# Two heads side by side on half-arrays, and another order of the late value products, in a windowed attention with a gated MLP on one core

## The chip, the cores and the metric

One core of a Trainium2 chip. The metric is the device time of one execution in microseconds; the median of three runs stands for a kernel. TensorE (PE) multiplies, PEld is its weight load, VectorE is DVE, ScalarE is ACT, GpSimd is POOL, and SyncE is SP, which issues the DMAs. A profiled execution has a span, a little shorter than its device time.

## The reference

```python
batch, n_heads, seq, head_dim = (4, 8, 768, 64); n_sink, window = (4, 128)     # q, k, v: float32
scores = (1 / sqrt(D)) * q @ k.T
keep = (pos_k < n_sink) | ((pos_q - pos_k >= 0) & (pos_q - pos_k < window))
scores = where(keep, scores, -1e9); scores -= max(scores)
a = exp(scores); a = a / (sum(a) + 1e-9)
x = (a @ v).transpose(0, 2, 1, 3).reshape(3072, 512)
h = x @ w_in            # w_in  [512, 2048]
g = h * cos(h)
out = g @ w_out         # w_out [2048, 512], float64 like w_in (it arrives as pairs of int32)
```

A query attends to the 128 keys up to its own and to the first four. Each row of 512 outputs of eight heads goes through the gated MLP.

## The kernel before

**Tiling.** The 3072 rows are cut in 12 chunks of 256 queries: first the four chunks that start a batch (`i0 == 0`), then the other eight. A chunk has eight heads, so there are 96 heads in order; the first 32 are called early. Early heads need no sinks of their own: their keys are the 256 of their own rows. The other 64, the late heads, see three blocks of 128 keys and 8 sink columns (`SW` = 136). Two chunks, 16 heads, make one dense pair of 512 rows: x in two float32r parts (`xhi`, `xlo`), three products each with `whi_in`, `wlo_in` into `h` (L476), the gate on ScalarE and VectorE, and three products into four accumulators (L521). There are six dense pairs of 16 slots, each slot 12 products of L476 and 12 of L521 with 512 moving columns.

**What runs beside what.** Heads 0 to 15 come first, alone. The first dense pair then runs among heads 16 to 31, the next four among 16 late heads each, and the last alone. While the first heads and the first dense pair run, the weights are loaded and turned from float64 pairs to float32 and split in two (`weight_piece`: L583, L589, L595 on VectorE, L616 on ScalarE, L619), through two raw buffers.

**An early pair of heads.** Two heads' q and k come in by DMA side by side, 64 columns each, and are turned on TensorE (`pe_turn`, L931) into one PSUM bank: head one on rows 0 to 63, head two on rows 64 to 127. `q_out` copies each head's 64 rows of q to its own half of `env.tqe`, whose other halves are zero (`early_q`, a memset); `k_out` copies both heads' k. `scores_pe` (L968) multiplies, in fp32, per head and query block, q with zeros on 64 of the 128 rows against the k of both heads: 128 columns for the first query block, 256 for the second. `mask` (L1046) adds the mask and takes the least, `expo` (L1055) exponentiates with a running sum, `denom` and `norm` divide the weights. `turn_early` (L1146) turns the three weight blocks of a head on TensorE, `p_out` copies them out of PSUM, and `values_pe` (L1191) multiplies them, in fp32, by v with 64 columns of zeros (`early_v`), so that both heads of a pair add into one 128-row tile. For the first 16 heads `split_early` takes x_hi from that tile, subtracts it inside PSUM with a product by minus the identity (L354) and copies the rest as x_lo. Heads 16 to 31 turn their weights in two steps and keep each head's 64 rows (`x_keep`).

**A late head.** Weights and v are split in float32r parts; `values` (L1215) makes seven products into `o.av`: the v operand has 128 columns (both parts) for the high weights and 64 for the low ones. The sinks of four heads are gathered by VectorE in `gc` (`sink_cols`, L1105, L1107), turned (L1120), and multiplied by 128 columns of sink values from `vs_part` (L1095, L1096). Rows 64 to 127 of the result are added to rows 0 to 63 (L1222, L1234).

**What sets the order.** Nothing is left to a run-time scheduler. Each step is added to a `Plan` with its engines and costs, its dependences, its buffers (`buf(tag, n)`) and a due time made of the constants in `C`. `Plan.order` goes through a model of the five engines once and emits the steps in a fixed order for each queue. A step with several engines listed goes to one of them there. PSUM has eight banks: `b0` to `b4`, `s`, `tp`, `av`.

## Time and profile before

| | |
|---|---|
| median of 3 runs | 727.12 us (726.59 to 727.43) |
| span of the profiled execution | 725.6 us |
| TensorE busy (records, tails in them) | 708.8 us, 3674 matmuls |
| VectorE, ScalarE, GpSimd busy | 599.3, 527.7, 127.5 us |
| first dense matmul | 55.7 us |
| TensorE clock granted | 1.00 of full speed in all stretches but the last |

The profiled execution's own time is its span and about 1.5 us around it: the median of the runs is 1.55 us above the span. Matmul records overlap: each one lasts from its start to the modelled end of the pipeline, so that the time a matmul takes from the engine is read from its start to the start of the next. An fp32 matmul leaves two records, a transpose or a float32r matmul one. Line numbers are those of the kernel before.

### The profile page before, as it was taken

The page shows a single profiled execution, that of the slowest core. Times are in us where ns is not written, and L with a number is a line of the kernel's source. Part 1 is how long each engine was busy: PE and PEld are TensorE (multiplying, and loading weights), DVE is VectorE, ACT ScalarE, POOL GpSimd, SP SyncE. Part 2 cuts the span into 40 slices and gives each one's busy share as a digit, 9 for nine tenths or more (in the row PEclk, how much of TensorE's full clock was granted, in tenths as well). Part 3 has the DMA queues.
Part 4 walks back from the last instruction along what each step waited for, and adds up shares of the span by engine and source line. Part 5 has one row for each costly group of instructions (what it writes and reads, how often), then busy time and mean ns, then how long its engine had stood idle before and what let it go on. Part 6 is the DMA issues. An engine that isn't in the chain of part 4 may idle for free.

```text
span 725.6 us, 12986 instructions
## 1 busy us (share of the span) xinstructions
PE 708.8 (98%) x3674; PEld 584.1 (81%) x3674; DVE 599.3 (83%) x1849; ACT 527.7 (73%) x1344; POOL 127.5 (18%) x213
## 2 busy tenths in 40 slices
PE   7998999999999999999999999999999999999996
PEld 7766787888888888888888888888888888888884
DVE  6889998988988978988978988878989865667762
ACT  3896976788697697796686886776887766566642
POOL 1010000001223222232231222232123222100000
PEclk9999999999999999999999999999999999999999
DMA  5665555533256333355433254433254500375551
GB/s 144 182 186 153 158 162 162 141 65 68 68 118 146 73 62 57 72 119 124 93 60 59 56 131 103 118 61 64 43 139 99 119 18 12 97 210 148 164 137 64
DMA packets 236501, 77.13 MB, mean 106 GB/s; under 512 B 221060, under 2 KB 221060, under 8 KB 236420
## 3 DMA queue, kind: packets, MB, share of 16 engines
q1 hardware_dynamic: 236128, 75.15, 43.4%
q10 hardware_dynamic: 292, 1.05, 0.5%
q8 instruction: 32, 0.52, 0.3%
q14 instruction: 49, 0.40, 0.2%
HBM read 69.86 MB, written 6.29 MB: 105 GB/s over the span
## 4 chain that ended last, share of the span: by engine, by line
PE 81%; ACT 11%; DVE 4%; issue 2%; DMA 1%; SPq 0%; ACTq 0%; DVEq 0%
PE acc L521 32%; PE h L476 32%; PE av L1215 5%; PE s L1024 4%; ACT p L1055 3%; PE s L968 2%; PE av L1191 2%; PE tp L1136 2%; ACT p L1073 1%; PE tp L1146 1%; PE qk L931 1%; ACT L485 1%; PE idle L1532 1%; ACT L1055 1%; ACT early L390 1%
## 5 line engine op out<-in xcount | busy, mean ns | idle before, releaser
L521 PE MATMUL acc<-whi_out,ghi 128*128 128x512 f32 x384 | 161.8, 421 | 0.0
L476 PE MATMUL h<-xhi,whi_in 128*128 128x512 f32 x384 | 155.2, 404 | 0.0
L476 PE MATMUL h<-xlo,whi_in 128*128 128x512 f32 x384 | 150.9, 393 | 0.0
L521 PE MATMUL acc<-whi_out,glo 128*128 128x512 f32 x384 | 150.8, 393 | 0.0
L521 PE MATMUL acc<-wlo_out,ghi 128*128 128x512 f32 x384 | 150.1, 391 | 0.0
L476 PE MATMUL h<-xhi,wlo_in 128*128 128x512 f32 x384 | 150.0, 391 | 0.0
L1174 POOL TENSOR_SCALAR_AFFINE_SELECT ph<-ph 128x512 fp32r<-128x512 f32 x128 | 87.4, 683 | 230.3 <-DVE ph L1167 226.4
L485 ACT ACTIVATE r<-h 128x512 f32<-128x512 f32 x96 | 57.1, 598 | 48.6 <-PE h L476 46.0
L476 PEld LDWEIGHTS h<-xlo,whi_in 128*128 128x128 f32 x384 | 72.1, 188 | 16.3
L521 PEld LDWEIGHTS acc<-whi_out,glo 128*128 128x128 f32 x384 | 72.1, 188 | 16.2
L476 PEld LDWEIGHTS h<-xhi,whi_in 128*128 128x128 f32 x384 | 72.2, 188 | 12.0 <-DVE r L498 0.3
L476 PEld LDWEIGHTS h<-xhi,wlo_in 128*128 128x128 f32 x384 | 72.4, 189 | 11.2
L521 PEld LDWEIGHTS acc<-whi_out,ghi 128*128 128x128 f32 x384 | 72.8, 190 | 10.7
L521 PEld LDWEIGHTS acc<-wlo_out,ghi 128*128 128x128 f32 x384 | 72.7, 189 | 9.4
L1055 ACT ACTIVATE p<-p,st 128x136 f32<-128x136 f32 (+1 forms) x192 | 79.2, 416 | 0.3
L498 DVE SCALAR_TENSOR_TENSOR r<-r,h 128x512 f32<-128x512 f32 x96 | 64.6, 674 | 16.9 <-ACT r L491 16.1
L506 ACT CAST ghi<-r 128x512 fp32r<-128x512 f32 x96 | 59.5, 619 | 22.8 <-PE acc L521 15.7
L512 DVE TENSOR_TENSOR glo<-r,ghi 128x512 fp32r<-128x512 f32 x96 | 66.3, 691 | 7.1 <-ACT ghi L506 6.3
L1046 DVE CUSTOM_DVE_ANT_0 p<-s,mk 128x136 f32<-128x136 f32 (+1 forms) x192 | 59.8, 313 | 6.5 <-PE s L968 3.1
L984 ACT CAST l<-tq 64x256 fp32r<-64x256 f32 x64 | 25.8, 403 | 46.7 <-PE s L1024 46.4
L1032 DVE COPY_PREDICATED s<-mk,s 128x128 f32<-128x128 int32 x128 | 37.3, 291 | 24.6 <-PE s L1024 22.5
L1024 PEld LDWEIGHTS s<-r,l 128*128 128x128 f32 x256 | 46.5, 188 | 12.3 <-DVE ph L1167 1.5
(153 smaller groups left out, 1302.3 us busy)
## 6 DMA issues: line engine op xcount, KB each, us to landing
xk<-in_k_dram SPq DMA_DIRECT2D x256, 48.0 KB
raw<-in_moe_w_out_dram SPq DMA_DIRECT2D x16, 512.0 KB
wt<-in_moe_w_in_dram SPq DMA_DIRECT2D x32, 256.0 KB
raw<-in_moe_w_in_dram SPq DMA_DIRECT2D x14, 512.0 KB
v<-in_v_dram SPq DMA_DIRECT2D x64, 96.0 KB
raw<-in_v_dram SPq DMA_DIRECT2D x32, 192.0 KB
out_dram<-wt SPq DMA_DIRECT2D x22, 256.0 KB
wt<-in_moe_w_out_dram SPq DMA_DIRECT2D x20, 256.0 KB
```

Of the source, the lines that this page charges most:

```text
L476: nc.tensor.matmul(out=o.h, lhsT=w[:, c, fs], rhs=xx[:, c, :], start=(c == 0 and n == 0), stop=(c == NC - 1 and n == 2),)
L485: nc.scalar.activation(out=o.r, in_=o.h, func=AF.Sin, scale=0.5)
L498: nc.vector.scalar_tensor_tensor(out=o.r, in0=o.r, scalar=0.5, in1=o.h, op0=ALU.subtract, op1=ALU.mult)
L506: nc.scalar.copy(out=o.ghi, in_=o.r)
L512: e.tensor_tensor(out=o.glo, in0=o.r, in1=f32(o.ghi), op=ALU.subtract)
L521: nc.tensor.matmul(out=y.acc[j], lhsT=gg[:, j * P : (j + 1) * P], rhs=w[:, f, :], start=(f == 0 and n == 0), stop=(f == NFT - 1 and n == 2),)
L1024: nc.tensor.matmul(out=o.s_ps[j][:, :w], lhsT=o.l[:, j * P : (j + 1) * P], rhs=r.rearrange("p n s -> p (n s)")[:, c0 : c0 + w], start=(n = ...
L1032: nc.vector.copy_predicated(out=o.s_ps[j][:, :P], mask=below.bitcast(I32), data=o.s_ps[j][:, SW : SW + P])
L1046: nc.vector.tensor_tensor_reduce(out=o.pj[j][:, :w], in0=o.s_ps[j][:, :w], in1=masks[min(o.i0 + j, 2)][:, :w], op0=ALU.add, op1=ALU.min, s ...
L1055: nc.scalar.activation(out=o.pj[j][:, :w], in_=o.pj[j][:, :w], func=AF.Exp, bias=o.lead.st[:, 0, o.nth, j : j + 1], scale=-1.0, accum_out= ...
L1174: nc.gpsimd.affine_select(out=ph[:, :, b, :], in_=f32(ph)[:, :, 1, :], pattern=[[0, 2 * CB], [(-1, 1)[b], P]], compare_op=(ALU.is_gt, ALU. ...
L1215: nc.tensor.matmul(out=dst, lhsT=lhs, rhs=rhs, start=(n == 0), stop=(n == len(seq) - 1), skip_group_check=True)
```

## The change

Early heads: the scores of two heads are issued as one step, alternating between the heads. Each uses the 64 rows of q and k that are its own, and each head's scores go to a PSUM bank of its own (`s` and `b0`, or `s` and `tp`). The values of two heads are one step too: v without zeros has 64 columns, and the two heads write partitions 0 to 63 and 64 to 127 of one bank. The zeros, their memsets and the two half copies of q go; q, k and v of a pair have two buffers each. x_lo is one subtraction on VectorE, in place of the product by minus the identity and a copy. Heads 16 to 31 turn their weights in one step and keep both heads' rows in one copy. The division of the weights is as before, ahead of the turn; its place in the plan and the cost given for the exponential of early heads change.

Late heads: the seven products come in another order, the sink values have 64 columns, with high and low parts on rows of their own (`odd16` marks the rows of the low part), and the sink columns are gathered twice, 32 for a head instead of 16. The sink values of a batch are loaded with eight DMAs instead of four.

All constants of the planner but a few are new, so that the order of nearly all steps can differ.

```diff
-    "ALT": 1.986, "BLF": 0.62, "CK": 43.221, "DA": -1.397, "DH": -1.402, "DM": -1.278, "DQ": 3.964, "DS": -6.226,
+    "ALT": 3.451, "BLF": 0.803, "CK": 48.478, "DA": -6.513, "DH": -5.89, "DM": -3.062, "DQ": 6.689, "DS": -21.639,
...
-    def x_lo(y, p, cs, early):
-        def fn(e):
-            if early:
-                copy(e, xlo[:, p, cs], y.f(p, cs))
-            else:
-                e.tensor_tensor(out=xlo[:, p, cs], in0=y.f(p, cs), in1=f32(xhi)[:, p, cs], op=ALU.subtract)
+    def x_lo(y, p, cs):
+        def fn(e):
+            e.tensor_tensor(out=xlo[:, p, cs], in0=y.f(p, cs), in1=f32(xhi)[:, p, cs], op=ALU.subtract)
...
-        m = add([("PE", 0.12)], x_minus(y, p, cs), [i], t + 0.3)
-        env.minus.users.append(m)
-        j = add([("ACT", act(NT, False)), ("DVE", dve(NT))], x_lo(y, p, cs, True), [m], t + 0.6)
+        j = add([("DVE", dve(NT))], x_lo(y, p, cs), [i], t + 0.6)
...
-                    for dup in range(2):
+                    for dup in range(4):
...
+        def q_out(o):
+            def fn(e):
+                o.tq = env.tqe[o.btq.nth]
+                copy(e, o.tq, o.qk[:, 0])
+            return fn
...
+        def scores_pe(pair):
+            oe = pair[0]
+
+            def fn(e):
+                for o in pair:
+                    t = ps.tile([P, 3 * P], F32, name=f"s_{o.tag}", tag=o.s_tag)
+                    o.s_ps = [t[:, : o.ws[0]], t[:, o.ws[0] : o.ws[0] + o.ws[1]]]
+                for j in range(CB):
+                    for o in pair:
+                        r = slice(o.odd * 64, o.odd * 64 + 64)
+                        c0 = max(o.i0 + j - 1 - o.kb0, 0) * o.sw
+                        nc.tensor.matmul(
+                            out=o.s_ps[j], lhsT=oe.tq[r, j * P : (j + 1) * P],
+                            rhs=oe.tk.rearrange("p n s -> p (n s)")[r, c0 : c0 + o.ws[j]], start=True, stop=True,
+                        )
+            return fn
...
+                e.tensor_copy(out=w, in_=o.vs32[r])
+                e.tensor_scalar(out=w, in0=f32(w), scalar1=odd16[r], scalar2=1.0, op0=ALU.mult, op1=ALU.mult)
+                e.tensor_tensor(out=w, in0=f32(w), in1=o.vs32[r], op=ALU.add)
...
+        def values_pair(pair, x):
+            oe = pair[0]
+
+            def fn(e):
+                av = x.f[oe.pair] = ps.tile([P, NT], F32, name=f"av_{oe.tag}", tag=oe.av_tag)
+                for n, (kb, qs) in enumerate(oe.cols):
+                    for o in pair:
+                        nc.tensor.matmul(
+                            out=av[o.odd * 64 : o.odd * 64 + 64, (qs[0] - oe.i0) * P : (qs[-1] + 1 - oe.i0) * P],
+                            lhsT=oe.v32[:, kb - oe.kb0, o.odd], rhs=o.pt[:, oe.offs[n] * P : oe.offs[n + 1] * P],
+                            start=(n == 0), stop=(n == len(oe.cols) - 1), skip_group_check=True,
+                        )
+            return fn
...
-                seq = [wide_hi]
-                if o.sj:
-                    lhs = sink_values()[:, o.pair, o.odd].rearrange("p a d -> p (a d)")
-                    seq.append((o.av[:, o.sj[0] * P :], lhs, gt[:, : len(o.sj) * P]))
-                seq += [*narrow[:2], wide_lo, *narrow[2:]]
+                sinks = o.av[:D], sink_values()[:, o.h // 4, o.pair % 2, o.odd], gt
+                seq = [
+                    block(0, o.phi, 2 * D), block(0, o.plo, D), sinks, block(2, o.phi, 2 * D),
+                    block(2, o.plo, D), block(1, o.plo, D), block(1, o.phi, 2 * D),
+                ]
...
-                r = slice(o.odd * 64, o.odd * 64 + 64)
-                copy(e, x.y.f(o.pair, slice(x.n * NT, x.n * NT + NT))[r], x.f[o.pair][r])
+                copy(e, x.y.f(o.pair, slice(x.n * NT, x.n * NT + NT)), x.f[o.pair])
...
-            o.s_tag = ("s", "b0") if g < GA else ("s", "s")
+            o.s_tag = ("s", "b0" if g < GA else "tp")[o.odd]
...
-                o.tp_tag, o.av_tag = "s" if o.comb else "tp", "tp"
+                o.tp_tag, o.av_tag = ("s", "tp") if o.comb else (("s", "tp")[o.odd], "s")
...
-                    bx, bb, o.btq = buf("xq", 1), buf(o.qk_tag, 1), buf("tqe", 1)
+                    bx, bb, o.btq = buf("xq", 1), buf(o.qk_tag, 1), buf("tqe", 2)
```

`block(n, t, w)` is the product of key block n by the weights `t` with the first w columns of its v operand.

## Rows read from the trace of the kernel before

**Rows 1.** The page: busy us (share), count; dense matmuls: busy us, mean ns.

```profile
PE 708.8 (98%) x3674; PEld 584.1 (81%) x3674; DVE 599.3 (83%) x1849; ACT 527.7 (73%) x1344; POOL 127.5 (18%) x213
...
L521 PE MATMUL acc<-whi_out,ghi 128*128 128x512 f32 x384 | 161.8, 421 | 0.0
```

**Rows 2.** Busy time by stretch of the span, all engines; then clock, DMA share, GB/s.

```profile
16.00:63.50 47.50, 43.87 (x256) 34.77 (x255) 42.31 (x142) 38.54 (x127) 3.48 (x5) 1.00 0.67 177
63.50:180.40 116.90, 115.16 (x573) 92.48 (x573) 107.55 (x292) 90.49 (x228) 2.55 (x7) 1.00 0.50 129
180.40:622.00 441.60, 440.42 (x2361) 366.56 (x2361) 376.41 (x1228) 337.99 (x876) 119.29 (x190) 1.00 0.38 83
...
sum 30.00, PE 27.78 PEld 21.38 DVE 26.68 ACT 28.22 POOL 2.48; mean PE 9.26 PEld 7.13 DVE 8.89 ACT 9.41 POOL 0.83
```

**Rows 3.** The chain that ended last, from 16 to 63.5 us, shares by line.

```profile
by line: PE s L968 13.8%; PE av L1191 12.3%; ACT early L390 8.4%; DMA raw<-in_moe_w_out_dram 7.9%; ACT p L1055 5.8%; PE qk L931 5.6%; DVE wt L589 5.4%; PE tp L1146 4.4%; ACT p L1073 4.2%; DVE wt L595 4.2%; issue 4.0%; PE idle L1532 3.5%; DV
```

**Rows 4.** Timeline of TensorE: one late head's values (start, duration; xN merges N records).

```profile
325.63 0.28 PE L1215 MATMUL av<-ph,vr 128*128 128x256 f32 x1
325.75 0.28 PE L1215 MATMUL av<-gt,x1r 128*128 128x256 f32 x1
325.87 0.22 PE L1215 MATMUL av<-ph,vr 128*128 128x128 f32 x1
...
325.92 0.40 PE L1215 MATMUL av<-ph,vr 128*64 128x128 f32 x3
325.99 0.40 PE L1215 MATMUL av<-ph,vr 128*64 128x256 f32 x3
326.10 0.28 PE L1215 MATMUL av<-ph,vr 128*128 128x128 f32 x2
326.16 0.22 PE L1215 MATMUL av<-ph,vr 128*64 128x128 f32 x1
326.22 0.45 PE L521 MATMUL acc<-whi_out,ghi 128*128 128x512 f32 x1
326.50 0.39 PE L521 MATMUL acc<-wlo_out,ghi 128*128 128x512 f32 x1
326.73 0.40 PE L521 MATMUL acc<-whi_out,glo 128*128 128x512 f32 x1
```

**Rows 5.** Groups by line and shape: busy us, mean ns, idle before; one DMA issue.

```profile
L1105 DVE CAST gc<-p 128x16 fp32r<-128x16 f32 x64 | 7.4, 174 | 1.9 <-ACT p L1073 1.9
L390 ACT COPY early<-qk 64x256 f32<-64x256 f32 x20 | 7.3, 366 | 11.0 <-PE qk L931 10.5
L390 ACT COPY early<-tp 128x384 f32<-128x384 f32 x13 | 6.2, 476 | 3.2 <-PE tp L1146 1.9 <-PE av L1191 1.2
L392 DVE COPY early<-tp 128x256 f32<-128x256 f32 x7 | 3.0, 421 | 0.4 <-PE tp L1146 0.4
...
1.31 0.46 SPq L923
```

**Rows 6.** Timeline of TensorE: an early head's scores and values among dense matmuls.

```profile
80.87 0.38 PE L968 MATMUL s<-tk,early 128*128 128x128 f32 x2
81.09 0.38 PE L1146 MATMUL tp<-ident,p 128*128 128x128 f32 x2
...
84.24 0.59 PE L968 MATMUL s<-tk,early 128*128 128x256 f32 x2
84.67 0.81 PE L1191 MATMUL av<-early,vpe 128*128 128x256 f32 x4
85.24 0.48 PE L476 MATMUL h<-xhi,whi_in 128*128 128x512 f32 x1
85.56 0.39 PE L476 MATMUL h<-xhi,wlo_in 128*128 128x512 f32 x1
```

**Rows 7.** Timeline of VectorE from 62 us, with the weight DMA it waits for.

```profile
62.45 0.43 DVE L583 TENSOR_SCALAR wt<-raw 128x512 int32<-128x512 int32 x1 [0.28 <-DMA raw<-in_moe_w_out_dram]
...
65.29 0.42 DVE L392 COPY early<-qk 64x256 f32<-64x256 f32 x1
```

More of the change, by code (lines that the diff above doesn't have):

```diff
@@ L1117, in fn @@
             def fn(e):
-                o.gp = late_bank(o, 2)[:GR]
-                for n, j in enumerate(o.sj):
-                    nc.tensor.transpose(
-                        out=o.gp[:, n * P : (n + 1) * P], in_=gc[:, j], identity=ident,
-                    )
+                o.gp = late_bank(o, 2)
+                for j in range(CB):
+                    nc.tensor.transpose(out=o.gp[:, j * P : (j + 1) * P], in_=gc[:, j], identity=ident)
             return fn
@@ L1408, in softmax @@
             ready = [i for _, o in group for i in o.msk]
-            ex = [
-                add(
-                    [("ACT", act(o.w[j]) + 0.19)], expo(o, j), ready, t + 1.02 * n + 0.01 * j, table="exp"
-                )
-                for n, (_, o) in enumerate(group) for j in range(CB)
-            ]
+            ex = []
+            for n, (_, o) in enumerate(group):
+                o.nm = [
+                    add(
+                        [("ACT", act(o.w[j]) + (0.0 if o.early else 0.19))], expo(o, j), ready, t + 1.02 * n + 0.01 * j,
+                        table="exp",
+                    )
+                    for j in range(CB)
+                ]
+                ex += o.nm
             t += 1.02 * (len(group) - 1) + 0.5
@@ new lines, in after_softmax @@
+            if o.early:
+                if o.odd == 0:
+                    return
+                pair = oe, _ = heads[g - 1], o
+                te = head_time(g - 1)
+                oe.bxv, bpt = buf("ve", 2), buf("phi", 1)
+                hold = [early[2:], [early_end]][g // 2] if g < 4 else []
+                v0 = add(dma(2), load_v_pair(oe), [oe.bxv, *hold], te - 2 * T + C["DV"] + 3.2, lat=2.4)
+                ready = [v0]
+                for m, w in enumerate(pair):
+                    pt = buf(w.tp_tag, 1)
+                    p0 = add([("PE", 0.107 * o.n)], turn_early(w), w.nm + [pt], head_time(g - 1 + m) + C["DA"] + 1.3)
+                    w.bp.users.append(p0)
+                    both = [("ACT", act(o.n * P, False)), ("DVE", dve(o.n * P))]
+                    p1 = add(both, p_out(w), [p0, ready[1] if m else bpt], head_time(g - 1 + m) + C["DA"] + 1.8)
+                    pt.users.append(p1)
+                    ready.append(p1)
+                bav = buf(oe.av_tag, 1)
+                y0 = add([("PE", 0.84)], values_pair(pair, x), [*ready, bav], te + C["DA"] + 5.0)
+                for bb in (oe.bxv, bpt, *early[2:]):
+                    bb.users.append(y0)
@@ L1616, in banded_path @@
             waiting.append((g, o))
-            if behind:
-                after_softmax(*behind.pop(0))
+            if behind and (behind[0][1].comb or o.odd != o.comb):
+                for _ in range(1 if behind[0][1].comb else 2):
+                    after_softmax(*behind.pop(0))
             if len(waiting) == o.nq:
```

298 lines of the change are left out of this document (118 added, 180 removed), and 12 rows, old and new, of the table C.

## The prediction

> **What bounds the kernel now.** I read the shares of the engines first, and they show TensorE busy for 98% of a span of 725.6 us [rows 1]. Busy time alone is no bound, since a matmul's record holds its pipeline's tail: the 512-column records of one group last 421 ns in the mean [rows 1], yet dense matmuls start 0.23 us apart [rows 4]. So I read start against start. The table of stretches [rows 2] cuts the kernel where the work changes. From 180.4 to 622 us TensorE is busy 440.42 of 441.60 us: there the last wait is always TensorE's own queue, and what a matmul group loses or gains there moves the end by as much. From 63.5 to 180.4 us, where the first dense pair runs among heads 16 to 31, TensorE is busy 115.16 of 116.90 and VectorE 107.55. From 16 to 63.5 us, heads 0 to 15 alone, no engine is: TensorE 43.87 of 47.50 with its tails and fillers, VectorE 42.31, ScalarE 38.54, but ScalarE takes 28.22 of the 30 us from 20 to 50 [rows 2]. The chain there goes from engine to engine: scores of L968 13.8%, values of L1191 12.3%, ScalarE's copies 8.4%, a weight DMA 7.9% [rows 3]. From 622 us on nothing of the change runs.
>
> **Late values (heads 32 to 95, 64 heads).** One head starts its products at 325.63, .75, .87, .92, .99, 326.10, .16, and the next dense matmul at 326.22, whose follower comes 0.28 later instead of 0.23 [rows 4]. That is 0.59 + 0.05 = 0.64 us. The steps are 0.12 after each 256-column matmul, 0.06 after a 128-column one whose successor has 64 weight columns, and 0.11 after the last one, whose successor has 128 (0.06 of it seen as start, 0.05 as the late follower). So a short matmul hides a 64-column weight load and not a 128-column one. The old order is wide, wide sink, 128, 64, 64, 128, 64: four steps of 0.12 and three of 0.06, 0.64 with rounding. The new order is 128 columns by 128 weights, 128 by 64, 256 sink columns by 64, 128 by 128, 128 by 64, 256 by 64, 256 by 128: steps 0.06, 0.06, 0.12, 0.06, 0.06, 0.12, 0.12, together 0.59. That is 0.055 less a head, 3.5 us for 64, all on TensorE's queue: **-3.5 us**. The bounds are 0, if the steps after the sinks follow their columns in some other way, and -4.5, if only the columns counted (1280 of them at 0.23 us for 512, 0.575 a head).
>
> The sinks' widening is paid on VectorE: 128 instructions for the sink columns, the casts at 174 ns, write 32 elements instead of 16 (from 16 elements at 174 ns to 256 at 421 it is 1.03 ns an element, so +17 ns each, 2.1 us), and there are 16 more instructions on the sink values, each at most a 256-column copy's 0.42, 6.7 us [rows 5]. VectorE has 65 us idle in that stretch [rows 2], which hides these 9; without that cover they would be at most +9. The four extra sink-value DMAs a batch take 0.46 us each of SP's queue [rows 5], 7.4 us over the whole stretch; queued behind them are only the key and query loads of heads some steps off. I cost them at nothing.
>
> **Scores and values of the first 32 heads (16 pairs).** These are full fp32, two records a matmul. A 128-column pair of records takes 0.22 us (80.87 to 81.09), a 256-column pair 0.43 (84.24 to 84.67) [rows 6], so 0.66 a head and 1.32 a pair of heads. The values of a head take 0.57 + 0.09 = 0.66 in the same rows, 1.31 a pair. The old kernel pads with zeros: 128 rows or columns of which 64 work. The new one issues as many columns, on half-arrays. No trace here has two matmuls on different halves, so I bound it. If nothing overlaps, the gain is 0. If everything does, 0.66 for each group. In between, matmuls start in order: the first head's two records follow each other on one half, the second head's first record can start only when the first head's second does, and so on. By passes of 0.11 and 0.22 the four matmuls then take 0.88. If moreover each 128-column weight load takes the 0.11 that it costs where it is not hidden [rows 4], one after the other, the scores take 1.10. I take 0.99 for scores (-0.33) and 0.88 for values (-0.43; their loads have 64 columns), nearest to the rows on in-order starts.
>
> From 63.5 to 180.4 us that is 7 pairs of scores and 8 of values, 2.3 + 3.4 = 5.7 us. VectorE is at 92% there and loses only copies: query copies 128 rows high instead of two of 64 (366 ns on ScalarE; 32 become 16), the kept values likewise (16 become 8), the transposed weights in one copy of 384 columns (476) instead of two, which saves one instruction's fixed 174 - 17 = 157 ns [rows 5]. Their ScalarE and VectorE time falls by some 16 x 0.37 + 8 x 0.37 + 16 x 0.16 = 11.4 us, 3 of it VectorE's in this stretch. Weight pieces hold VectorE back too: at 62.45 and again before 65.3 it stands in line behind a raw weight DMA, and a query copy behind it [rows 7]. So I give 80%: **-4.6 us**.
>
> From 16 to 63.5 us scores are 6.6 and values 5.8 us of the chain; a quarter and a third of them is 3.5. ScalarE, the fullest engine from 20 to 50, loses half of its 64-row query copies (1.7 us) and, to VectorE, the low halves of x. The subtraction by matmul (L354) goes as well. Against it, the first mask of a pair now waits for both heads' scores and the values for both heads' weights, about 0.5 us later each; the second query and key buffer lets the next pair start ahead of that. I take **-3 us**, bounds 0 and -6. The memsets and the x_lo moved to VectorE lie in gaps there, at nothing. The new priorities reorder everything; I know no sign for that, and allow 4 us either way.
>
> Sum: 3.5 + 4.6 + 3.0 = 11.1. The profiled span of 725.6 us becomes 714.5. The median of the runs is 1.5 us above that span, so the forecast is **716.0 us**.
>
> **The rule that speaks against it.** The rows of a late head switch four times between matmuls of 128 and of 64 weight columns, and the steps of 0.06 leave no room for a stall [rows 4]. The Trainium skill, TensorEngine Tiling (Array Packing), section Key Properties, says that a change of tiling mode drains TensorE. For column widths at one position this case's trace disagrees; for row halves, and for a second column position, no run here shows it. By that rule the time would be the slower rival's, 735; by the rows on widths it would be the sum's.
>
> **Rivals.** (1) *The halves overlap fully* or the new order closes the idle time as well: 0.66 for each group, -1.3 a pair. Eight pairs among the dense work give 8 to 10, the first 16 heads 5 to 6, the late values 3.5: about 709. For it: different halves share no weights; against it: starts in order, and ScalarE at 94% in the first stretch. (2) *Halves run one after the other*: the change doesn't do what it says. Then -3.5 from the late values and 1 to 2 from the copies remain: 722. For it: fp32 takes two records each, which no row shows overlapped. (3) *VectorE becomes the bound* between 63.5 and 180.4: with 92% there, and the weight conversions in its queue ahead of the masks, the early gain is lost and the late extra 9 us on VectorE delay some scores: 724 to 727. (4) *Slower: a drain at every switch.* Two fp32 records of 128 columns, 0.11 apart, end 0.38 after the first one's start, 0.16 after the next group may start [rows 6], so a drain costs up to 0.16, and 0.12 for a load that can't be hidden [rows 4]: 0.28. Each pair switches four times (into and out of row halves, into and out of column halves), 1.1 us. With the overlap lost too, eight pairs add 9 among the dense work and up to 5 in the first stretch; less 3.5 and 1.5 of the copies, about 735. It decides from 0.19 us a switch on, where it eats the pair's 0.76, and turns the whole slower from about 0.25.
>
> **How the numbers follow.** Forecast (partial overlap, 711 to 720) 0.47; rival 1 0.17; rival 2 0.13; rival 3 0.11; rival 4 0.12. Slower by over 0.2% (728.6 on; about what a measurement can tell from no change) is rival 4 and a little of rival 3: 0.13. Within 0.2%: part of rival 3, 0.05. Faster: 0.82. Leaving out the far ends of rivals 1 and 4, the range is 706 to 727.5.
>
> **What would show it.** Late values: the sum of steps per head 0.59 instead of 0.64, the sink matmul 128*64. Early scores and values: starts of the second head's records beside the first's, and a pair's four matmuls in 0.9 to 1.1 us and 0.9; a drain would stand as a gap of 0.15 us or more ahead of the first record of a group and behind its last. Stretches: heads 0 to 15 shorter by 3, the first dense pair by 4 to 5, each later dense pair by 0.9. I am wrong if the early groups take 1.3 us a pair, or if VectorE's idle time between 63 and 180 us goes to nothing while TensorE waits.

## The result, and the profile after

The changed kernel takes 731.1 us (median of 4 runs, 729.6 to 731.9) against 726.9 for the kernel before on the same chip: ratio 1.0058, 95% interval 1.0044 to 1.0072. It is 4 us slower, where the prediction had it 11 us faster. Its profiled span is 727.9 us. The page's shares, then the table of stretches, cut at the first matmuls of the first, second and sixth dense pair (us, then busy time and count of PE, PEld, DVE, ACT, POOL, granted clock, DMA share, GB/s):

```profile
PE 699.0 (96%) x3666; PEld 555.5 (76%) x3666; DVE 600.8 (83%) x1844; ACT 523.5 (72%) x1335; POOL 129.1 (18%) x200
...
16.00:51.50 35.50, 27.83 (x199) 18.02 (x197) 27.35 (x110) 30.00 (x106) 2.34 (x5) 0.95 0.64 167
51.50:167.40 115.90, 113.19 (x588) 82.79 (x589) 104.75 (x270) 88.67 (x212) 5.77 (x8) 1.00 0.55 145
167.40:624.60 457.20, 449.34 (x2388) 365.82 (x2387) 396.84 (x1282) 344.92 (x905) 119.77 (x178) 1.00 0.39 84
```

Against [rows 1, 2]: TensorE is busy for 10 us less in a longer span. The 0.95 in the first row is a fall of the granted clock to 0.74 (part of it at 1.2 GHz) from 45 to 51.5 us, behind 5 us with TensorE busy for 3.67; before shows 1.00 there. What that costs is not shown; behind it the clock is 1.00 in both. The first dense pair starts at 51.5 us instead of 55.7, and the second at 167.4 instead of 180.4. The sixth starts at 624.6 instead of 622.3. So the change is ahead by 13.0 us at the second dense pair, and the stretch behind it, which the prediction called TensorE-bound, takes 457.2 instead of 441.9 us and gives all of it back. Of the 13.0, 4.5 are work that only moved: behind the second pair's start stand 15 more output matmuls of 0.231 us and 8 more late scores. The real lead is 8.5.

To follow the rest I use one number, **TensorE's idle between pairs**: over all matmuls from the second dense pair's first to the sixth's, the time between two starts less the step that the matmul's form shows (0.45 ns a column, from 0.23 us for 512, or 0.92 ns a column of the next weights where that is more, from 0.12 us for 128; [rows 4]). It is 2.6 us before and 16.7 after. A change in the third digit of these two rates moves all of these sums together by about 1 us; the differences between kernels stay. The account closes: +4.5 moved, -3.5 late products, +14.1 idle make +15.1, and 15.3 were measured.

What the prediction said of the late values came. One late head's values (timeline of TensorE):

```profile
330.49 0.40 PE L514 MATMUL acc<-whi_out,glo 128*128 128x512 f32 x1
330.73 0.28 PE L1192 MATMUL av<-ph,vr 128*128 128x128 f32 x2
330.85 0.28 PE L1192 MATMUL av<-gt,vs 128*64 128x256 f32 x1
330.96 0.52 PE L1192 MATMUL av<-ph,vr 128*128 128x128 f32 x4
331.32 0.39 PE L514 MATMUL acc<-whi_out,ghi 128*128 128x512 f32 x1
```

330.73 to 331.32 is 0.59 us, and the follower comes in the usual 0.23. An early pair's scores and values (the first line of each group merges all eight records of two heads; the line of x2 is a narrow window at the group's start):

```profile
81.77 0.40 PE L514 MATMUL acc<-whi_out,glo 128*128 128x512 f32 x1
82.10 0.38 PE L954 MATMUL s<-early 64*128 64x128 f32 x2
...
82.10 0.93 PE L954 MATMUL s<-early 64*128 64x128 f32 x8
82.95 0.49 PE L469 MATMUL h<-xhi,whi_in 128*128 128x512 f32 x1
83.29 0.39 PE L469 MATMUL h<-xhi,wlo_in 128*128 128x512 f32 x1
...
89.02 0.40 PE L514 MATMUL acc<-whi_out,glo 128*128 128x512 f32 x1
89.35 0.87 PE L1167 MATMUL av<-early,early 128*64 128x256 f32 x8
90.15 0.50 PE L469 MATMUL h<-xhi,whi_in 128*128 128x512 f32 x1
90.49 0.39 PE L469 MATMUL h<-xhi,wlo_in 128*128 128x512 f32 x1
```

The two heads' records start 6 to 7 ns apart (0, 6, 213, 220, 325, 331, 543, 550 ns from the group's first): the halves overlap fully. But the dense matmul ahead of the group holds the queue for 0.33 us instead of 0.23, and so does the one behind it. From dense start to dense start, less two dense steps, a pair's scores take 1.52 - 0.46 = 1.06 us and its values 1.01, where the kernel before takes 1.32 and 1.31 [rows 6].

All six score groups between dense matmuls take 1.06. Of the eight value groups there only four take 1.01. In the others the second head's first record stands 0.04 to 0.66 us behind the first head's, because its weights are still being copied out of PSUM, and they take 1.04, 1.30, 1.42 and 1.66; the mean of the eight is 1.18. The longest, with the copy it waits for:

```profile
163.54 1.52 PE L1167 MATMUL av<-early,early 128*64 128x256 f32 x8
163.60 0.54 DVE L385 COPY early<-tp 128x384 f32<-128x384 f32 x1
165.00 0.50 PE L514 MATMUL acc<-whi_out,ghi 128*128 128x512 f32 x1
```

### The profile page after: what moved, and what is told of

Its sections match the earlier page's. It is cut to its first block, busy times and chain, and to the rows that moved or that the text cites. A ratio compares the mean times of both kernels' runs of the same rounds, so it can differ in the third digit from the quotient of the medians.

```text
span 727.9 us, 12978 instructions
## 1 busy us (share of the span) xinstructions
PE 699.0 (96%) x3666; PEld 555.5 (76%) x3666; DVE 600.8 (83%) x1844; ACT 523.5 (72%) x1335; POOL 129.1 (18%) x200
## 4 chain that ended last, share of the span: by engine, by line
PE 73%; ACT 10%; DVE 9%; DMA 3%; issue 3%; SPq 1%; DVEq 0%; ACTq 0%
PE h L469 29%; PE acc L514 28%; PE s L1010 4%; PE av L1192 4%; ACT p L1041 3%; DMA xk<-in_k_dram 2%; PE tp L1120 2%; PE s L954 1%; PE idle L1506 1%; ACT p L1059 1%; DMA xq<-in_q_dram 1%; ACT early L383 1%; DVE glo L505 1%; DVE p L1032 1%; SPq L877 1%
## 5 line engine op out<-in xcount | busy, mean ns | idle before, releaser
L514 PE MATMUL acc<-whi_out,ghi 128*128 128x512 f32 x384 | 155.5, 405 | 0.0
L1154 POOL TENSOR_SCALAR_AFFINE_SELECT ph<-ph 128x512 fp32r<-128x512 f32 x128 | 90.0, 703 | 237.5 <-DVE ph L1147 213.3
L478 ACT ACTIVATE r<-h 128x512 f32<-128x512 f32 x96 | 57.1, 597 | 79.2 <-PE h L469 50.5
L505 DVE TENSOR_TENSOR glo<-r,ghi 128x512 fp32r<-128x512 f32 x96 | 68.7, 716 | 6.5 <-ACT ghi L499 5.0
L1010 PEld LDWEIGHTS s<-r,l 128*128 128x128 f32 x256 | 44.3, 188 | 22.5 <-issue 6.8
L1010 PE MATMUL s<-r,l 128*128 128x264 f32 x256 | 55.7, 298 | 3.0 <-DVE st L1032 1.5
```

The source lines that it names most:

```text
L478: nc.scalar.activation(out=o.r, in_=o.h, func=AF.Sin, scale=0.5)
L505: e.tensor_tensor(out=o.glo, in0=o.r, in1=f32(o.ghi), op=ALU.subtract)
L514: nc.tensor.matmul(out=y.acc[j], lhsT=gg[:, j * P : (j + 1) * P], rhs=w[:, f, :], start=(f == 0 and n == 0), stop=(f == NFT - 1 and n == 2),)
L1010: nc.tensor.matmul(out=o.s_ps[j][:, :w], lhsT=o.l[:, j * P : (j + 1) * P], rhs=r.rearrange("p n s -> p (n s)")[:, c0 : c0 + w], start=(n = ...
L1154: nc.gpsimd.affine_select(out=ph[:, :, b, :], in_=f32(ph)[:, :, 1, :], pattern=[[0, 2 * CB], [(-1, 1)[b], P]], compare_op=(ALU.is_gt, ALU. ...
```

## The experiments

The idle column is the number explained above; starts are of the first matmul of a dense pair. Both come from the one profiled execution of a kernel, which lies up to 2 us from the median of its runs (e3 2.2 below, e7 2.0 above), while the ratios go by all runs.

| kernel | ratio to before (95%) | 1st | 2nd | 6th | idle |
|---|---|---|---|---|---|
| before | 1 | 55.7 | 180.4 | 622.3 | 2.6 |
| after | 1.0058 (1.0044, 1.0072) | 51.5 | 167.4 | 624.6 | 16.7 |
| e1_old_consts | 1.0407 (1.0386, 1.0427) | 54.2 | 179.2 | 651.1 | 35.6 |
| e2_new_consts | 1.0081 (1.0056, 1.0106) | 53.1 | 175.6 | 627.4 | 8.5 |
| e3_late_old | 0.9996 (0.9984, 1.0008) | 50.5 | 166.2 | 620.1 | 9.9 |
| e4_late_new | 1.0072 (1.0052, 1.0092) | 57.7 | 182.6 | 628.0 | 9.5 |
| e5_vector_only | 1.0101 (1.0078, 1.0124) | 57.8 | 182.0 | 628.7 | 7.1 |
| e6_tensor_only | 0.9989 (0.9977, 1.0000) | 55.8 | 180.4 | 621.3 | 5.3 |
| e7_mixed_consts | 1.0052 (1.0031, 1.0073) | 51.4 | 171.0 | 624.3 | 13.2 |
| e8_mixed_consts_order | 1.0294 (1.0268, 1.0319) | 52.2 | 176.6 | 641.7 | 25.4 |
| e9_dma_only | 1.0045 (1.0031, 1.0060) | 58.4 | 183.3 | 626.7 | 4.0 |
| e10_one_op_more | 1.0040 (1.0025, 1.0054) | 55.4 | 180.3 | 625.8 | 6.1 |
| e11_after_short | 1.0024 (1.0013, 1.0035) | 53.5 | 169.6 | 625.2 | 15.2 |
| e12_late_short | 1.0028 (1.0017, 1.0038) | 56.6 | 180.9 | 623.7 | 6.9 |
| e13_before_moved | 0.9999 (0.9990, 1.0008) | 55.2 | 179.8 | 621.7 | 2.5 |
| e14_after_moved | 1.0040 (1.0026, 1.0055) | 50.7 | 167.1 | 625.6 | 18.0 |
| e15_late_old_moved | 0.9990 (0.9979, 1.0002) | 52.2 | 168.4 | 621.7 | 9.3 |
| e16_after_short_moved | 1.0029 (1.0018, 1.0041) | 50.6 | 166.9 | 622.1 | 14.8 |
| e17_head_by_head | 1.0079 (1.0062, 1.0096) | 53.3 | 169.9 | 627.8 | 17.5 |
| e18_old_order | 1.0084 (1.0066, 1.0102) | 52.3 | 168.3 | 626.8 | 14.4 |

### Which part: constants, early halves, late part

Four kernels cross the parts of the change. Theory A of these expectations: the new operations gain and the new constants lose; theory B: the constants are fitted to the operations, and the late part loses.

**Old constants under the new operations** (e1), and **new constants over the old operations** (e2; the cut shows e1, e2 is the same edit the other way):

```diff
-    "ALT": 3.451, "BLF": 0.803, "CK": 48.478, ...
+    "ALT": 1.986, "BLF": 0.62, "CK": 43.221, ...
```

> The changed kernel with the planner's constants of the kernel before; the operations are all those of the change. The changed kernel's gain of 13 us up to the start of dense pair two is lost in the four dense pairs among late heads, which take 115 us each instead of 112.2. Theory A (order): the new constants put late instructions into TensorE's queue ahead of their data; with the old ones a late dense pair takes 111.3 us (112.2 less 16 x 0.055) and the time is 715 to 719. Theory B (sinks): the sink gather of 32 columns and the longer sink values hold VectorE up, and TensorE waits for the turned sinks; the late dense pairs stay at 114 to 115 and the time is 726 to 731.

> The kernel before with the planner's constants of the changed one; no operation differs from before. Theory A (order): the late dense pairs take about 115 us here too, and the time is 735 to 745. Theory B (sinks): they stay at 112 to 113, and the time is 725 to 729.

Both expectations on e1 failed: 757.7 us. The old constants don't fit the new steps at all; TensorE idles 35.6 us. e2 gave 733.1, between its two ranges: **the new constants alone cost 5.9 us** (ratio 1.0081) on the old operations. It is ahead by 4.8 us at the second dense pair, about 4 of it moved work, and then idles 5.9 us more than before.

**The late operations of before in the changed kernel** (e3), and **the late part alone in the kernel before** (e4); both keep the order of their plan:

```diff
-                    for dup in range(4):
+                    for dup in range(2):
...
-                sinks = o.av[:D], sink_values()[:, o.h // 4, o.pair % 2, o.odd], gt
+                    seq.append((o.av[:, o.sj[0] * P :], lhs, gt[:, : len(o.sj) * P]))
```

(The cut shows e3; e4 is the same edit the other way.)

> The changed kernel with the late heads' operations of before (16 sink columns a head, sink values 128 columns wide, products in the old order), in the same order of the plan's steps as in the changed kernel. Theory A (order): the late dense pairs take 115.5 to 116 us, the stalls stay and the 0.9 us of the products comes on top; 733 to 736. Theory B (sinks): the stalls go, the pairs take 112.2, and the time is 719 to 722.

> The kernel before with the late heads' operations of the change alone (32 sink columns, sink values of 64 columns, new order of the products), in the same order of the plan's steps as before. The prediction's term: 64 x 0.055 = 3.5 us less, 723.4, late dense pairs of 111.3. Theory A agrees with that. Theory B (sinks): VectorE is late for the turned sinks, stalls of 1 us or more at L1120's successor eat the gain, 726 to 735.

The late part, which was to bring 3.5 us, costs 5.2 us in the plan of before (ratio 1.0072) and about 4.5 in the new plan (1.0058 against 0.9996). e3's 727.2 lies in neither of its ranges; e4's 733.2 is in theory B's. The early halves are the difference between e3 and e2, -6.2 us. So the whole is about +5.9 constants, -6.2 early halves, +4.5 late part, each to within 1 to 2 us by the intervals. This split holds for this order of the steps alone: under the new operations the old constants cost 25 us more than the new ones (e1 against the changed kernel).

### Why the late part loses: VectorE and SyncE, or TensorE

e5 is the kernel before with the late part's work on VectorE and SyncE only (16 sink-value DMAs a batch instead of 8, as in the changed kernel). e6 has its work on TensorE only and leaves out the low part of the sink values.

```diff
+                e.tensor_copy(out=w, in_=o.vs32[r])
+                e.tensor_scalar(out=w, in0=f32(w), scalar1=odd16[r], scalar2=1.0, op0=ALU.mult, op1=ALU.mult)
+                e.tensor_tensor(out=w, in0=f32(w), in1=o.vs32[r], op=ALU.add)
```

```diff
+                sinks = o.av[:D], sink_values()[:, o.pair, o.odd, 0], gt
+                seq = [
+                    block(0, o.phi, 2 * D), block(0, o.plo, D), sinks, block(2, o.phi, 2 * D),
```

> The kernel before, its plan kept in its order, with only the late part's work on VectorE and SyncE: the sink columns gathered 32 to a head instead of 16, the sink values made in three operations on 32 rows instead of two on 16, eight value DMAs a batch instead of four. TensorE's late products stay as they were. Before: 727.2. Theory V (the wider VectorE work stands in the path of the late dense pairs, because VectorE's queue is served in order): 730 to 733, with about 1 us more for each late dense pair. Theory S (VectorE's idle time hides it, and what the late part lost comes from TensorE's new order): 726.5 to 728.

> The kernel before, its plan kept in its order, with only TensorE's side of the late part: the seven products of a late head in the new order and the sinks 64 columns wide. The sink values enter with their high part alone (their low part is left out), so that VectorE works as before. Before: 727.2. If TensorE's queue alone sets the late stretch, as my prediction had it, 64 heads times 0.055 come out: 723.5. Theory W (the late stretch is held by VectorE and ScalarE as much, and TensorE's saved time turns into waits): 726 to 727.5, with 2 us or more of new waits on TensorE between 180 and 622 us.

The work on VectorE and SyncE costs 7.3 us, a little more than theory V's range, though it adds only 5.4 us of busy time to VectorE in the stretch, which has 65 us idle [rows 2]. TensorE's part brings 0.8 of its 3.5 (0 to 1.7 by its interval): idle rises by 2.7. Both theories of waiting (V and W) hold: 7.3 - 0.8 is e4's loss within its interval. Part of e6's new idle stands before the transposes of the late heads (before, then e6; the last column is idle time and what ended it):

```profile
L1136 PE MATMUL tp<-ident,p 128*128 128x128 f32 x128 | 25.6, 277 | 1.2 <-DVE st L1046 0.8
...
L1136 PE MATMUL tp<-ident,p 128*128 128x128 f32 x128 | 25.8, 278 | 2.0 <-DVE st L1046 1.1 <-ACT p L1073 0.7
```

Set slot against slot, e5 falls behind the kernel before in one place per late dense pair: the starts of its third pair's slots 0 to 3 are late by 2.64, 2.62, 3.62 and 3.77 us, and then the lag stands until the next pair. There VectorE's queue reads, in the kernel before (first fence; its 0.66 and 0.73 fall beside a GpSimd mask that runs for 1.73 us from 296.15) and in e5 (second):

```profile
296.59 0.66 DVE L1095 CAST x1r<-yt 16x128 fp32r<-16x128 f32 x1
297.28 0.73 DVE L1096 TENSOR_TENSOR x1r<-yt,x1r 16x128 fp32r<-16x128 f32 x1
297.94 0.28 DVE L1032 COPY_PREDICATED s<-mk,s 128x128 f32<-128x128 int32 x1
...
298.79 0.22 DVE L1095 CAST x1r<-yt 16x128 fp32r<-16x128 f32 x1
299.04 0.28 DVE L1096 TENSOR_TENSOR x1r<-yt,x1r 16x128 fp32r<-16x128 f32 x1
```

```profile
301.62 0.22 DVE L1101 CAST x1r<-yt 32x128 fp32r<-32x128 f32 x1
301.87 0.28 DVE L1102 TENSOR_SCALAR x1r<-x1r,neg 32x128 fp32r<-32x128 f32 x1
302.19 0.28 DVE L1103 TENSOR_TENSOR x1r<-x1r,yt 32x128 fp32r<-32x128 f32 x1
...
303.97 0.29 DVE L1103 TENSOR_TENSOR x1r<-x1r,yt 32x128 fp32r<-32x128 f32 x1
304.29 0.29 DVE L1038 COPY_PREDICATED s<-mk,s 128x128 f32<-128x128 int32 x1
```

The sink values stand directly ahead of the masks of a late head (`s`), and every instruction more moves the mask, the softmax and the transposes behind it. TensorE's row 1.2 us later, a late head's transposes:

```profile
305.52 0.41 PE L1141 MATMUL tp<-ident,p 128*128 128x128 f32 x2 [0.59 <-DVE st L1052]
```

The other 2 us of e5 are lost before its first dense pair. The next three kernels take the pieces one by one: e9 doubles the sink-value DMAs alone, e10 adds one VectorE instruction a head to the sink values, and e12 is e4 with two instructions a head and 8 DMAs a batch (its cut is against e4).

```diff
-                    for dup in range(2):
+                    for dup in range(4):
```

```diff
                 e.tensor_copy(out=w[r, :, h, 0, :], in_=o.vs32[r])
+                e.tensor_scalar(
+                    out=w[r, :, h, 0, :], in0=f32(w)[r, :, h, 0, :], scalar1=1.0, scalar2=1.0, op0=ALU.mult, op1=ALU.mult
+                )
```

```diff
-                e.tensor_scalar(out=w, in0=f32(w), scalar1=odd16[r], scalar2=1.0, op0=ALU.mult, op1=ALU.mult)
-                e.tensor_tensor(out=w, in0=f32(w), in1=o.vs32[r], op=ALU.add)
+                e.scalar_tensor_tensor(
+                    out=w, in0=f32(w), scalar=odd16[r], in1=o.vs32[r], op0=ALU.mult, op1=ALU.add
+                )
```

> The kernel before with one edit: 16 sink-value DMAs a batch instead of 8 on SyncE's queue (they fill rows that nothing reads). The vector-only kernel has 16 of them in the first 30 us, where before has 8, and its TensorE then waits 2.4 us for query loads; its first dense pair starts at 57.8 instead of 55.7. Theory Q (SyncE's queue: the extra DMAs stand ahead of the query and key loads of heads 4 to 8, which nothing hides): first dense pair at 57 to 58, total 728.5 to 729.5 against 727.2, no loss in the late dense pairs. Theory N (the queue has room, as my prediction had it): 727.

> The kernel before with one edit: the sink values of a head are made with three VectorE instructions instead of two (a multiplication by one between them), so 4 more instructions of some 0.3 us a batch, 16 in the whole stretch; DMAs and gather as before. In the vector-only kernel each late dense pair falls back at one place, 1.0 to 1.15 us between its first and fourth slot, where these instructions stand ahead of a mask in VectorE's queue. Theory P (the place decides: no slack there): 1.0 to 1.3 us for each of the four late dense pairs, total 731 to 732.5. Theory G (the wider gather costs the rest, the sink values little): 727.5 to 729.

> The kernel before with the late part alone (as e4_late_new, 733.2), sink values again in two instructions and 8 DMAs a batch. The late part then keeps TensorE's new order and the wider gather. If the sink values' instructions and DMAs made the whole loss, it comes to where TensorE's order alone came, 726 to 727. If the gather costs something by itself: 728 to 730.

e10: 4 instructions of 0.3 us a batch cost 1.0 us in each of the last three of the four late dense pairs and 0.6 in the first, 3.5 us in the profiled execution and 2.9 by the ratio, just under theory P's range. Most of the instructions' 1.2 us a batch comes out, although their engine is idle for 15% of the stretch. e12, with them and half of the DMAs gone, is back from 1.0072 to 1.0028. The 2 us that are left fit its second expectation, a price of the wider gather itself: 0.9 us are there at the first dense pair, 0.8 come in the late pairs, and no run takes them further apart.

e9 costs 3.3 us, more than expected. Its profiled execution shows 2.7 before the first dense pair, and 1.5 in the late pairs, which the expectation had ruled out. SyncE's queue in the kernel before, then in e9, and TensorE's wait behind it there:

```profile
10.27 3.74 SPq L858 DMA_DIRECT2D yt<-in_v_dram  x8
14.53 0.91 SPq L923 DMA_DIRECT2D xq<-in_q_dram  x2
...
10.29 6.64 SPq L858 DMA_DIRECT2D yt<-in_v_dram  x16
17.03 0.91 SPq L923 DMA_DIRECT2D xq<-in_q_dram  x2
...
19.63 0.41 PE L931 MATMUL qk<-ident,xq 128*128 128x128 f32 x2 [2.25 <-DMA xq<-in_q_dram]
```

The kernel before issues 8 there in 3.74 us and goes on with the query loads at 14.5; the changed one issues 16 in 6.18 us and goes on at 16.8. These loads are for the first late batch, whose first cast of sink values runs at 187 us in e5. Behind the wait the granted clock is lower as well: in e9 TensorE is busy 2.68 of 5 us from 15 to 20, and is granted 0.66 from 20 to 25 (part of it at 1.2 GHz); in the kernel before it is busy 4.92 and then granted 1.00. In e12 the 8 DMAs that read 8 rows four times take 5.55 us, so it saved only 0.6 to 1 us of queue.

### The same pieces in the changed kernel

e11 is the changed kernel with e12's edit. e13 to e16 issue the first late batch's loads behind those of the early heads (the kernel before, the changed one, e3, and the changed one with 16 loads and two instructions).

```diff
         steps = plan.order(True)
+        kd = next(n for n, s in enumerate(steps) if "load_batch_v" in s[2].__qualname__)
+        kv = next(n for n, s in enumerate(steps) if "vs_part" in s[2].__qualname__)
+        steps.insert(kv - 500, steps.pop(kd))
```

> The changed kernel, same plan, with the sink values made in two instructions a head instead of three (cast, then multiply-and-add in one) and loaded by 8 DMAs a batch instead of 16 (each fills the 32 rows of a head from 8 rows read four times). If the sink values' queue places are what the late part lost: 1 us back at the start and about 1.1 us in each of four late dense pairs, 731.1 becomes 725 to 726.5. If the loss is elsewhere (the 64-column order, the gather): 730 to 731.

> The kernel before with one edit: the 8 sink-value loads of the first late batch, which stand at 10.3 to 14.0 us in SyncE's queue, are issued behind the loads of the early heads (some 80 us later), all else in the same order. Theory Q (they hold up the query loads there): the reverse of the dma-only kernel, the first dense pair 1 to 2 us earlier than 55.7, total 725.5 to 726.5 against 727.4. Theory N (only the second eight of them cost anything): 727 to 728.

> The changed kernel with the same edit: its 16 sink-value loads of the first late batch (10.55 to 16.7 us in SyncE's queue) are issued behind the loads of the early heads, all else in the same order. Theory Q: the first dense pair starts at 48.5 to 50 instead of 51.5, and 1.5 to 3 us of the whole come out: 728 to 729.5 against 731.1. Theory N: 731.

> The early part of the change with the late operations of before (727.2 so far), and its 8 sink-value loads of the first late batch moved in the same way. Theory Q: 1 to 2 us come out, 725 to 726.5, which would be a version below both kernels. Theory N: 727.

> The changed kernel with its 16 loads moved and the sink values made in two instructions a head instead of three. If the loads' place and the sink values' instructions are additive: 1.5 to 3 us from the first and 1 to 1.5 from the second (four late dense pairs at 0.35, as the changed kernel with short sink values showed), 726.5 to 728.5. What is then left against 727.4 is the constants' late plan (about 5 us) against the early halves' gain (about 6). If the loss is elsewhere: 730 to 731.

The pieces are real in this plan too, but smaller. e11 comes to 1.0024 and e16 to 1.0029 from 1.0058, some 2 us of the 4.5; both lie between the ranges of their expectations, and e16, with all sixteen loads out of the way, is no better than e11. e13 shows that the first eight loads cost nothing (0.9999): without them the query loads go out at 12.9 us instead of 14.5, and nothing comes of it; only the second eight reach past that cover. Moving all 16 (e14) puts the first dense pair 0.8 us earlier, but by the sixth pair the profile is 1.0 us behind the changed kernel's, and the ratios (1.0040 and 1.0058) overlap. So the gain of 1.5 to 3 us that theory Q expected of e14 is not shown. e15 is the best version that was run with the whole computation, at 0.9990 (0.9979, 1.0002): not told from the kernel before, nor from e3.

What is left of the late part's loss in the new plan, some 2.5 us (1.0029 against 0.9996), is not settled. The gather of four heads takes 0.80 us there and 0.70 in e3 where no mask is beside it, but that this is the price is not shown.

### The constants

e7 plans early heads and the first dense pair by the new constants and the rest by the old ones (on e3's operations); e8 takes the old ones for the weights between queues as well.

```diff
+        def use(late):
+            nonlocal T
+            C.update(CL if late else CE)
```

> The early part of the change with the late operations of before (as e3_late_old, 727.2), planned with the new constants for heads 0 to 31 and the first dense pair, and with the constants of before for the late heads and the dense pairs behind; the parameters that weigh one engine's queue against another's are the new ones. If the new constants cost their 5.6 us in the late stretch alone, the first dense pairs keep their new starts (about 50.5 and 166) and the late dense pairs fall back from 113.6 to 112.2: 718 to 722. If the constants cost it as a set, and not by stage: 725 or more.

> The same mixture of constants, but with the parameters that weigh the queues from before as well. If the late stretch's loss comes with these parameters: 716 to 720, below the mixture that keeps the new ones. If they matter only to the early heads: slower than that mixture, 724 to 735, with the first dense pair's start later than 51.

Neither gain came: 1.0052 and 1.0294. In e7 one dense pair, the third, idles for 8 us, in e8 the third to the fifth for 7 to 9 us each; which steps wait there was not followed. e7 lies where its second case had it (constants as a set), e8 beyond both of its cases. Where the new ones lose is seen in e3, after and e16 alike, for instance here (after: VectorE, then TensorE):

```profile
347.39 0.87 DVE L1090 CAST gc<-p 128x32 fp32r<-128x32 f32 x4
348.18 0.92 DVE L1095 TENSOR_TENSOR gc<-p,gc 128x32 f32<-128x32 f32 x4
...
347.89 0.39 PE L469 MATMUL h<-xlo,whi_in 128*128 128x512 f32 x1
349.25 0.41 PE L1108 MATMUL gp<-ident,gc 128*128 128x128 f32 x2 [0.97 <-DVE gc L1095]
349.41 0.47 PE L469 MATMUL h<-xhi,whi_in 128*128 128x512 f32 x1
```

The transposes of the sink columns (`gp`) stand in TensorE's queue ahead of dense matmuls that are ready, and wait 1.0 us for VectorE's gather. e3 has the same row with 1.07. Five such places make 4.6 of the 16.7 us of idle after and 3.9 of e3's 9.9; the late scores make 5.2 and 4.0; before has neither above 0.15 us.

Four of the five stand where the gather falls beside a mask on GpSimd. There it takes 1.7 us instead of 0.8 (after), or 1.6 instead of 0.7 (e3), so 0.9 us of such a wait goes with the mask. In e2, the new constants over the old operations, one gather of the sixteen falls beside a mask, and it is the only one that TensorE waits for (VectorE, GpSimd, TensorE):

```profile
267.09 0.84 DVE L1105 CAST gc<-p 128x16 fp32r<-128x16 f32 x4
267.85 0.87 DVE L1107 TENSOR_TENSOR gc<-p,gc 128x16 f32<-128x16 f32 x4
...
267.25 1.36 POOL L1174 TENSOR_SCALAR_AFFINE_SELECT ph<-ph 128x512 fp32r<-128x512 f32 x2 [3.64 <-DVE gc L1105]
...
268.77 0.43 PE L1120 MATMUL gp<-ident,gc 128*112 128x128 f32 x2 [0.95 <-DVE gc L1107]
```

In e2 the gather makes 1.1 us and the late scores 3.0. So by themselves the constants cost more at the late scores than at the gather; that gather and mask meet in every late pair is seen only where the early halves are there as well.

### The halves and the products' order

e17 is the changed kernel with the four matmuls of a pair issued head after head; e18 has the products of a late head in the old order.

```diff
-                for j in range(CB):
-                    for o in pair:
+                for o in pair:
+                    for j in range(CB):
```

```diff
-                    block(0, o.phi, 2 * D), block(0, o.plo, D), sinks, block(2, o.phi, 2 * D),
-                    block(2, o.plo, D), block(1, o.plo, D), block(1, o.phi, 2 * D),
+                    block(1, o.phi, 2 * D), sinks, block(0, o.phi, 2 * D), block(0, o.plo, D),
+                    block(1, o.plo, D), block(2, o.phi, 2 * D), block(2, o.plo, D),
```

> The changed kernel with one edit: in the early scores and values the four matmuls of a pair are issued head after head instead of taking turns between the heads. My prediction's theory (matmuls start in order, so the second head's first record can start only when the first head's second matmul has): the scores then take 0.88 to 1.1 us of starts instead of 0.65, a pair loses 0.2 to 0.45 in each group, and the 8 pairs among dense work cost 3 to 7 us: the first late dense pair starts that much later, total 732 to 737 against 731. Rival: the queue runs ahead and both halves work side by side in any order: 731.

> The changed kernel with one edit: the seven products of a late head in the order of before (256, sinks, 128, 128, 256, 128, 128 columns), the sinks still 64 columns wide. The steps of a head then sum to 0.65 us instead of 0.59. If TensorE's queue sets the end of the late stretch, 64 times 0.06 come on top: 734.5 to 735. If the late stretch is held by the other engines' order as well, as the tensor-only kernel showed (1.0 us of 3.5 came out): 731.5 to 732.5.

In e17 a group is no longer (TensorE; x2 is again a narrow window at its start):

```profile
98.10 0.40 PE L514 MATMUL acc<-whi_out,glo 128*128 128x512 f32 x1
98.43 0.39 PE L954 MATMUL s<-early,early 64*128 64x128 f32 x2
...
98.43 0.93 PE L954 MATMUL s<-early,early 64*128 64x128 f32 x8
99.29 0.50 PE L514 MATMUL acc<-whi_out,ghi 128*128 128x512 f32 x1
99.63 0.40 PE L514 MATMUL acc<-wlo_out,ghi 128*128 128x512 f32 x1
```

The second head's first record starts 13 ns behind the first head's, although both matmuls of the first head, four records, stand ahead of it in the queue. So halves don't start in the order of issue, and my step on in-order starts falls: a group takes 1.06 us in either order. The whole is 1.0079, an interval (1.0062, 1.0096) that overlaps the changed kernel's. It lies in the range of the theory that fell, without its mechanism: of a lag of 1.7 us at the first dense pair, 0.5 is there at the first group of scores and 1.3 at the second (17.74 us against 16.41), ahead of any dense work. TensorE is busy 2.88 of 5 us from 45 to 50, and the granted clock is 0.50 from 50 to 55, all of it at 1.2 GHz. The lag is 2.6 us once that stretch is over, 2.4 at the second pair, so that the eight pairs among dense work add nothing, and 3.2 at the sixth.

e18 costs 1.9 us against the changed kernel (1.0084 to 1.0058; 0.2 to 3.6 us by the two intervals), about half of 64 x 0.06: the late stretch gives back only a part of what TensorE's queue saves, as in e6.

## Why the prediction was wrong

**Right: the late values' steps, and the size of the early lead.** Late values 0.59 us a head. Scores gained 0.26 a pair (0.33 predicted). Values gained 0.30 (0.43 predicted) in the four groups that had both heads' weights in time, and 0.13 in the mean of the eight. The first dense pair starts 4.2 us earlier (3 predicted), and the second a further 8.8, of which 4.5 only moved; the other 4.3 stand against 4.6 predicted. That is partly luck: seven pairs of scores and eight of values give 2.9 by these figures, where the prediction had 5.7 and took 80% of it, and the rest is not traced to a part. In all the lead is 8.5 us, where the sum had 7.6.

**Right for two wrong reasons: the halves.** I took partial overlap from starts in order, and no drain. The overlap is full (rival 1's mechanism), and a switch costs 0.2 us in the mean (rival 4's): 1.06 less the 0.65 that one head's records take is 0.41 for two, 0.10 of it ahead of the group, 0.10 behind its first record, and 0.20 from its last record to the follower of the next dense matmul. By luck the two errors nearly cancel in the scores. Rival 4 needed a lost overlap to make the kernel slower. The Trainium skill, TensorEngine Tiling (Array Packing), section Key Properties, says that a change of tiling mode drains TensorE. For row halves and a second column position the trace of after agrees, with these 0.2 us a switch; for 128 and 64 weight columns at one position it still shows none (steps of 0.06).

**The step that failed: "there the last wait is always TensorE's own queue, and what a matmul group loses or gains there moves the end by as much".** TensorE's busy 440.42 of 441.60 us [rows 2] does not say that. When TensorE gets ahead, its next steps wait for VectorE and ScalarE, whose queues are as fixed as its own: of 3.5 us saved, 0.8 reach the end in the old plan, and 2.7 turn into idle (e6).

**The step that failed with it: "VectorE has 65 us idle in that stretch [rows 2], which hides these 9".** Idle time is a sum over the stretch, and the 16 instructions on the sink values stand at places without any: 2.9 us for them (e10). The forecast named +9 as the cost without that cover; 7.3 is what VectorE's and SyncE's work cost together (e5). Rival 3 came nearest: in it "the late extra 9 us on VectorE delay some scores". But it also has the early gain lost, and that gain came; and it goes no higher than 727.

**The DMAs.** The text on the change has eight sink-value DMAs a batch instead of four, and I counted 4 more; they are 16 instead of 8. The sentence that behind them are "only the key and query loads of heads some steps off" doesn't hold for the first batch. Its loads stand at 10 us ahead of loads of the first heads, where the query load behind them was late by 2.25 us (e9).

**The constants: "I know no sign for that, and allow 4 us either way".** They cost 5.9 us on the old operations (e2), more than the margin, and the range's upper end held no share of it together with the late loss. The sum with what the runs showed: -6.2 early halves, +5.9 constants, +4.5 late part, +4.2 measured.

What stays open: which of the constants puts the gather beside a mask and the late scores where TensorE waits for them, and some 2.5 us of the late part in the new plan.

## What to carry to other kernels

An engine that is busy 99% of a stretch is not the only bound there: before an edit on another engine is costed at nothing, look at the places in its queue where its instructions will stand, and at what is next behind them, not at the sum of its idle time. A saving on the busiest engine of a statically ordered kernel reaches the end only as far as the engines behind it can follow; measure one part alone in the old order to learn that share. A retuned plan is an edit of its own with a price of its own: run it once over the old operations.

## What the runs showed of the hardware

- Matmuls in full fp32 on two different row halves, or on two column halves, overlap fully when the operands of both are ready: records of the two heads start 6 to 7 ns apart when the heads take turns in the queue (after), and 13 to 14 ns apart when one head's two matmuls are issued ahead of the other's (e17).
- Into and out of such a group the neighbouring 512-column matmul holds the queue for 0.33 us instead of 0.23, and a group loses 0.41 us (scores) or 0.36 (values) at its two borders. Float32r matmuls that alternate between 128 and 64 weight columns at one position show no such step (0.06 us).
- DMA issue on SyncE: 16 small loads of 8 rows by 2 x 64 took 6.18 us, 8 such loads 3.74 us, and 8 loads of 32 rows that read 8 rows four times 5.55 us (after, before, e12).
- VectorE's gather of the sink columns is slower beside a GpSimd mask. Of the sixteen gathers of eight instructions after, the four that fall beside one take 1.70 to 1.71 us, the other twelve 0.79 to 0.91; in e3 four take 1.62 to 1.63 and twelve 0.69 to 0.84. No run moves one gather away from a mask with all else equal. Two gathers after, the second with the mask beside it (its VectorE lines stand in the section on the constants):

```profile
205.77 0.40 DVE L1090 CAST gc<-p 128x32 fp32r<-128x32 f32 x4
206.07 0.49 DVE L1095 TENSOR_TENSOR gc<-p,gc 128x32 f32<-128x32 f32 x4
...
347.55 1.40 POOL L1154 TENSOR_SCALAR_AFFINE_SELECT ph<-ph 128x512 fp32r<-128x512 f32 x2 [1.57 <-DVE ph L1147]
```
